# Chunked linear attention feeding an FFN: from 128-position blocks to two halves of 64 with a state at the chunk's middle

## Chip, cores and metric

The kernel runs on one NeuronCore of a Trainium2 chip. The metric is device time in microseconds (us) of one execution. Engines: PE (TensorE matmul; PEld is its weight load), DVE (VectorE), ACT (ScalarE), POOL (GpSimd), SP (which issues most DMAs). Lnnn is a line of the kernel; where nothing else is said, of the kernel before.

## What is computed

Gated linear attention over 4 batches, 8 heads, 768 positions and 48 features, then a multiplicative FFN on the 3072 tokens of 384 features:

```
for t in range(S):
    state = alpha[:, :, t, :, None] * state + einsum('bhd,bhe->bhde', k[:, :, t], v[:, :, t])
    y[:, :, t] = einsum('bhd,bhde->bhe', q[:, :, t], state)
x = y.transpose(0, 2, 1, 3).reshape(B * S, H * D)
out = ((x @ w1) * (x @ w2)) @ w3 @ w_out
```

The weights come as 64-bit floats and are converted on the chip.

## The kernel before

The sequence is cut into chunks of 128 positions: 6 per batch (NCH), 24 in all (N). Inside a chunk the decay is taken into q and k by cumulated logarithms: `logs` (L315, ACT), `decays` (L338: cumulated sums on PE, then two exponentials on ACT, L363/L364), `decayed` (L371, one multiplication on DVE, L373: qk = kq * e). `transposed` (L384) turns q and k by 16 transposes on PE (L395) and two copies on ACT (L397, tile qkT). Heads go in four pairs j, with i the head of a pair.

Chunks from 8 on are called turned (L161). For such a chunk n the work on PE is:
- `scores(n)` -> `turned_scores` (L435): k'q in both 64-position halves and from the first half to the second; 16 products, 8 of them 128 columns wide and 8 of them 64 (L443). Between them stand the low values of chunk n-1 (L432), 8 products of 64 rows. Four mask operations on DVE (L453) bring the scores to SBUF (tile ms).
- `attend_state(n)` (L476): q times the state T before the chunk, both halves of the positions, 16 products of 48 rows and 64 columns (L485) into two PSUM banks y. The first chunk of a batch has no state.
- `attend(n)` (L498): the second half's values, 8 products of 128 rows (L508) onto y[0]; three copies on ACT (L505 twice, L510) to x, which SP stores to DRAM (xd).
- `outer(n)` (L400): k'v over all 128 rows, 8 products (L407); DVE adds the old state (L417) for the new one. A batch's last chunk has none. `advance` (L419) multiplies every second state by a decay on POOL (L426).
- `turn_v` (L164): POOL copies half of v to the other partitions (tile vt), for the products that write across the halves.

Loop iteration n (L756 to L863) works on chunk n's scores, chunk n-1's values and chunk n+1's transposes, in the order: state of n-1, scores of n with low values of n-1, transposes of n+1, values of n-1, outer products of n. After these follow pieces of the FFN's gate from a queue (`run`, L718): a piece is `exact` (L584), nine products into two banks (L581), with an activation on ACT (L590) and an operation on DVE (L592); two pieces make a gate, and DVE then multiplies both (L629). Also in the iteration: weight conversion (`convert`, L246 to L269, on ACT and DVE), the sums for chunk n+3 (L357), and L334, an operation on logarithms on DVE. In iterations 9, 13, 17, 21 no gate pieces run; `split_early` (L554; L548 on ACT, L549 and L551 on DVE) splits the FFN's next input into three parts, which the next gate pieces read.

A gate's products multiply parts 0 and 1 into the first bank, part 2 into the second. From about 181 us on, attention is over and PE works on the rest of the gate, the folding of w3 and w_out, and the projection.

The framework takes instructions in the order in which the functions issue them and sorts each engine's queue itself by its own estimates; `issue_after` marks only bound this order. The queue is fixed when the kernel is built. An engine runs its own queue in order and waits on semaphores for others. PSUM has 8 banks, given out by `bank()` as earlier users finish.

Of the kernel before, what the change touches and what calls it, by code (L numbers as in the profile page):

```python
# [12 lines left out]
I32 = mybir.dt.int32  # L13
# [35 lines left out]
def kernel(  # L49
# [77 lines left out]
    vts = [p1.tile([C, NP, DP], FP32, name=f"vt{i}") for i in range(2)]  # L127
    for x in vts:
        nc.gpsimd.memset(x[:, :, D:], 0.0)
# [66 lines left out]
    keep_turned = p1.tile([C, 2, DP], I32, name="keep_turned")  # L196
    qks = [p1.tile([C, 2, H, DP], FP32, name=f"qk{i}") for i in range(3)]
    Ts = [p1.tile([C, NP, DP], FP32, name=f"T{i}") for i in range(2)]
    decs = [p1.tile([C, LINE // 2], FP32, name=f"dec{i}")[:, 0:3 * NP].rearrange("p (m j) -> p m j", m=3) for i in range(2)]
# [10 lines left out]
    for half in range(2):  # L210
        nc.gpsimd.tensor_copy(out=keep_turned[ds(DP * half, DP), 1 - half], in_=keep[ds(DP * half, DP), ds(DP * half, DP)])
    nc.gpsimd.memset(keep_turned[DP:, 1], -1)
# [12 lines left out]
    for x in Ts + decs:  # L225
        nc.gpsimd.memset(x, 0.0)
# [202 lines left out]
    def attend_low(n, j, i):  # L429

        s, w = ds(DP * i, DP), (vts[n % 2][:, j, :] if i else st["v", n][:, 2 * j, :])
        nc.tensor.matmul(st["y", n][1][ds(DP * (1 - i), DP), j, :], w[s], st["ms", n][s, i, j, 0:DP],  # L432
                         start=(n % NCH == 0 and j == 0), stop=(j == NP - 1), skip_group_check=True)

    def turned_scores(n):  # L435

        qkT = st["qkT", n]
        sc = [bank().rearrange("p (j c) -> p j c", j=NP) for _ in range(2)]
        for j in range(NP):
            for part in range(2):  # L440
                for i in range(2):
                    r, t = ds(DP * i, D), slice(DP * part, C)
                    nc.tensor.matmul(sc[i][ds(DP * (part ^ i), DP), j, t], qkT[r, 0, j, ds(DP * part, DP)],  # L443
                                     qkT[r, 1, j, t], start=True, stop=True)
            if turned(n - 1):
                for i in range(2):
                    attend_low(n - 1, j, i)
        ms = work.tile([C, 2, NP, C], FP32, tag="ms", name="ms")
        for i in range(2):
            r = ds(DP * i, DP)  # L450
            low, high = (keep_turned[r, 0], keep_turned[:, 1]) if i else (keep[r, 0:DP], keep[:, DP:])
            for x, mask, t in ((slice(DP * i, DP * (i + 1)), low, slice(0, DP)), (slice(0, C), high, slice(DP, C))):
                masked = nc.vector.tensor_tensor(ms[x, i, :, t].bitcast(I32), sc[i][x, :, t].bitcast(I32),  # L453
                                                 mask[:, None, :].to_broadcast([x.stop - x.start, NP, DP]),
                                                 op=ALU.bitwise_and)
        ends_of_part1[0] = mark["ms", n] = masked.ins
        st["ms", n] = ms

    def scores(n):
        if turned(n):  # L460
            return turned_scores(n)
# [14 lines left out]
    def attend_state(n):  # L476
        qkT = st.pop(("qkT", n))
        if turned(n):
            y = st["y", n] = [bank()[:, 0:NP * DP].rearrange("p (j c) -> p j c", c=DP) for _ in range(2)]
            if n % NCH:  # L480
                for j in range(NP):
                    for t in range(2):
                        for i in range(2):
                            r = ds(DP * i, D)
                            nc.tensor.matmul(y[t][ds(DP * (i ^ t), DP), j, :], Ts[n % 2][r, j, :],  # L485
                                             qkT[r, 1, j, ds(DP * (1 - t), DP)],
                                             start=(j == 0), stop=False, skip_group_check=True)
            return
# [9 lines left out]
    def attend(n):  # L498
        y, ms, vc = st.pop(("y", n)), st.pop(("ms", n)), st.pop(("v", n))
        to = xd.rearrange("(h i d) t -> i d h t", i=2, d=D) if turned(n) else xd.rearrange("(b h d) t -> b d h t", b=2, d=D)  # L500
        if turned(n):
            x = work.tile([C, NP, C], FP32, tag="x", name="x", bufs=4)
            with after_marks(*[("qkT", n + 2)] * (n + 2 < N)):
                for i in range(2):
                    nc.scalar.copy(x[ds(DP * i, DP), :, 0:DP], y[1][ds(DP * (1 - i), DP)])  # L505
            for j in range(NP):
                for i in range(2):
                    nc.tensor.matmul(y[0][ds(DP * i, DP), j, :], vts[n % 2][:, j, :] if i else vc[:, 2 * j, :], ms[:, i, j, DP:],  # L508
                                     start=(n % NCH == 0 and j == 0), stop=(j == NP - 1), skip_group_check=True)
            copied = nc.scalar.copy(x[:, :, DP:], y[0])  # L510
# [245 lines left out]
    for n in range(N + 1):  # L756
# [17 lines left out]
        late_state = early_pair(n - 1)  # L774
        if n and not late_state:
            attend_state(n - 1)
        if n < N:
            scores(n)
            if late_state:
                attend_state(n - 1)  # L780
        else:
            for j in range(NP):
                for i in range(2):
                    attend_low(n - 1, j, i)
        transposed(n + 1)
# [33 lines left out]
        with after_marks(*[("vt", n)] * turned(n)):  # L819
            advance(n)  # L820
# [3 lines left out]
        if n:  # L824
            attend(n - 1)
        outer(n)
# [15 lines left out]
        run(pieces > 1)  # L842
# [14 lines left out]
        turn_v(n + 1)  # L857
# [98 lines left out]
```

## Time and profile before

| what | value |
|---|---|
| runs | 455.81, 455.42, 460.12 us; median 455.81 |
| profiled execution, its own time | 455.61 us |
| its span | 453.9 us |
| granted PE clock, mean over the span | 1.00 |
| scores L443 | 512 instructions, 33.0 us of PE |
| masks L453 | 64 on DVE, 26.6 us |
| copies of v L167 | 32 on POOL, 15.5 us |

A product of 32-bit floats counts as two PE instructions in the rows (x32 is 16 products); a transpose counts as one. Durations of PE rows overlap: what a group costs is the distance from its start to the next group's start. The same holds, less strongly, for DVE and ACT: the next operation starts some 0.08 to 0.12 us before the listed end of the one before. Times within the profile are counted from the span's start.

### The profile page before, as it was taken

What the parts mean: (1) busy time and instruction counts of PE and PEld (TensorE: products, weight loads), DVE (VectorE), ACT (ScalarE), POOL (GpSimd) and SP (SyncE); (2) the same over time, 40 slices, a digit from 0 to 9 for tenths busy, and PEclk for the clock granted to TensorE, in tenths of its full rate; (3) what the DMA queues carried; (4) which work ended last, traced back from release to release, by engine and by line L of the source; (5) the groups of instructions that cost most, each with busy time, mean ns of one, the idle gap of its engine ahead of it and who ended that gap; (6) DMA issues with size and microseconds to landing.
All of it is one profiled execution on the core that took longest, in us unless ns stands there. A gap on an engine that the chain in (4) does not pass through costs nothing.

```text
span 453.9 us, 11111 instructions
## 1 busy us (share of the span) xinstructions
PE 439.3 (97%) x4304; PEld 390.9 (86%) x4304; DVE 370.0 (82%) x600; ACT 278.4 (61%) x523; POOL 85.1 (19%) x171
## 2 busy tenths in 40 slices
PE   4998999999999999999999999999999999999996
PEld 2766898898989978888888888888888999999996
DVE  2799997999979898989999999999427576777671
ACT  4778956878688573978865766575435333333430
POOL 6334341225116330021121010100010000000000
PEclk9999999999999999999999999999999999999999
DMA  8999999989999952465775263610139565565411
GB/s 202 271 227 250 239 243 244 210 203 223 211 216 194 276 168 95 153 187 179 243 232 186 94 201 105 205 48 23 48 101 271 173 183 161 167 190 175 150 49 52
DMA packets 149381, 79.98 MB, mean 176 GB/s; under 512 B 97184, under 2 KB 138784, under 8 KB 149328
## 3 DMA queue, kind: packets, MB, share of 16 engines
q1 hardware_dynamic: 143840, 64.84, 54.2%
q0 software_dynamic: 5488, 14.43, 9.8%
q8 instruction: 34, 0.56, 0.5%
q14 instruction: 19, 0.16, 0.1%
HBM read 57.19 MB, written 22.06 MB: 175 GB/s over the span
## 4 chain that ended last, share of the span: by engine, by line
PE 87%; DVE 6%; DMA 3%; ACT 2%; issue 1%; SPq 0%; DVEq 0%
PE bank L581 73%; PE bank L395 2%; PE bank L443 2%; PE bank L508 2%; PE bank L485 2%; PE bank L407 1%; DVE qk L373 1%; DMA x3b<-xd 1%; PE bank L432 1%; DVE ms L470 1%; PE bank L357 1%; DMA abd<-r 1%; PE bank L354 1%; DMA xd<-x 1%; DMA ac<-in_alpha_dram 1%
## 5 line engine op out<-in xcount | busy, mean ns | idle before, releaser
L581 PE MATMUL bank<-x,w 128*128 128x512 f32 (+1 forms) x688 | 161.6, 372 | 0.4 <-ACT e L364 0.2
L581 PEld LDWEIGHTS bank<-x,w 128*128 128x128 f32 x688 | 124.4, 188 | 19.5 <-issue 0.7
L581 PE MATMUL bank<-w3o,ab 128*128 128x384 f32 x576 | 100.2, 334 | 0.0
L581 PEld LDWEIGHTS bank<-w3o,ab 128*128 128x128 f32 x576 | 99.9, 188 | 0.2
L581 PE MATMUL bank<-x3b,w 128*128 128x512 f32 (+1 forms) x248 | 71.6, 384 | 0.0
L606 ACT ACTIVATE bank<-bank 128x512 f32<-128x512 f32 (+1 forms) x72 | 40.9, 570 | 30.7 <-PE bank L581 30.6
L581 PEld LDWEIGHTS bank<-x3b,w 128*128 128x128 f32 x248 | 46.3, 188 | 8.5 <-ACT x L505 0.4
L655 POOL DMA_DIRECT2D abd<-r x33 | 19.3, 585 | 138.8 <-DVE r L641 116.5
L705 DVE TENSOR_TENSOR ab<-abl,ab 128x1024 fp32r<-128x1024 f32 x24 | 29.4, 1226 | 14.9 <-ACT ab L704 14.9
L590 ACT ACTIVATE t<-bank 128x384 f32<-128x384 f32 x24 | 11.8, 492 | 45.5 <-PE bank L581 45.5
L704 ACT ACTIVATE ab<-abl 128x1024 fp32r<-128x1024 f32 x24 | 25.4, 1060 | 22.6 <-PE bank L581 20.1
L397 ACT COPY qkT<-bank 128x512 f32<-128x512 f32 x48 | 25.9, 593 | 20.0 <-PE bank L395 20.0
L581 PE MATMUL bank<-wo,w3T 128*128 128x384 f32 x192 | 36.3, 337 | 0.0
L581 PEld LDWEIGHTS bank<-wo,w3T 128*128 128x128 f32 x192 | 34.1, 188 | 1.2
L592 DVE SCALAR_TENSOR_TENSOR o<-bank,t 128x384 f32<-128x384 f32 x24 | 13.4, 558 | 25.4 <-issue 14.0
L252 ACT ACTIVATE power<-power,rebias 128x512 uint32<-128x512 uint32 (+1 forms) x36 | 25.0, 695 | 13.8 <-DVE power L250 13.8
L373 DVE TENSOR_TENSOR qk<-kq,e 128x768 f32<-128x768 f32 x24 | 23.1, 962 | 9.0 <-ACT e L364 8.8
L641 DVE TENSOR_TENSOR r<-bank,r 128x512 f32<-128x512 f32 x32 | 21.8, 682 | 9.3 <-PE bank L581 8.6
L706 DVE SCALAR_TENSOR_TENSOR ab<-ab,abl 128x1024 fp32r<-128x1024 f32 x24 | 29.2, 1219 | 0.0
L592 DVE SCALAR_TENSOR_TENSOR r<-bank,r 128x384 f32<-128x384 f32 (+1 forms) x40 | 22.7, 577 | 6.5 <-ACT r L590 4.9
L590 ACT ACTIVATE r<-bank 128x384 f32<-128x384 f32 (+1 forms) x40 | 20.5, 515 | 9.5 <-PE bank L581 8.1
L254 DVE SCALAR_TENSOR_TENSOR mant<-mant,raw 128x512 f32<-128x512 uint32 (+1 forms) x36 | 23.5, 652 | 2.9 <-ACT raw L246 2.9
(119 smaller groups left out, 744.6 us busy)
## 6 DMA issues: line engine op xcount, KB each, us to landing
abl<-abd SPq DMA_DIRECT2D x24, 512.0 KB, 4.3
abd<-r POOLq DMA_DIRECT2D x33, 256.0 KB, 3.5
raw<-in_moe_w_dram SPq DMA_DIRECT2D x64, 128.0 KB, 4.1
raw<-in_moe_w_dram SPq DMA_DIRECT2D x12, 512.0 KB, 4.9
kq<-in_k_dram SPq DMA_DIRECT2D x24, 192.0 KB, 5.0
kq<-in_q_dram SPq DMA_DIRECT2D x24, 192.0 KB, 4.8
xd<-x SPq DMA_DIRECT2D x48, 96.0 KB, 3.6
xT<-xd POOLq DMA_DIRECT2D x6, 768.0 KB, 5.4
```

Of the source, the lines that this page charges most:

```text
L252: nc.scalar.activation(power, power, AF.Relu, scale=2.0 ** 23, bias=rebias)
L254: nc.vector.scalar_tensor_tensor(mant, top, 2.0 ** -20, rest, op0=ALU.mult, op1=ALU.add)
L373: mark["qk", n] = nc.vector.tensor_mul(qks[n % 3][:, :, :, 0:D], st.pop(("kq", n)), st.pop(("e", n)).rearrange("p i (h d) -> p i h d", h=H ...
L397: mark["qkT", n] = nc.scalar.copy(qkT[:, :, :, ds(DP * half, DP)], tp[half]).ins
L581: nc.tensor.matmul(p, w[part][i], x[part][i], start=start and part == parts[0] and i == 0, stop=stop and part == parts[-1] and i == n - 1, ...
L590: mark["scale"] = nc.scalar.activation(t, p1, AF.Copy, scale=(1.0 + 1.0 / P) * scale).ins
L592: nc.vector.scalar_tensor_tensor(to, p2, scale, t, op0=ALU.mult, op1=ALU.add)
L606: mark["scale"] = nc.scalar.activation(p, p, AF.Copy, scale=1.0 + 1.0 / P).ins
L641: nc.vector.tensor_mul(r[0], p, r[0])
L704: nc.scalar.activation(t[:, 0], ab, AF.Copy, scale=1.0 - 2.0 ** -13)
L705: nc.vector.tensor_sub(t[:, 1], ab, t[:, 0].bitcast(FP32))
L706: nc.vector.scalar_tensor_tensor(t[:, 2], t[:, 0].bitcast(FP32), -1.0 - 1.0 / P, ab, op0=ALU.mult, op1=ALU.add)
```

## The change

From chunk 8 on the chunk is treated as two halves of 64 positions, each with its own state before it. `outer_halves` makes k'v for the first and the second half apart (16 products of 64 rows into two banks, 8 for a batch's last chunk). `middle` adds the first to T for the state at the chunk's middle, U, and the second to U for the next T, both on DVE. `half_scores` needs scores only inside each half: 16 products of 64 columns, two masks of 128x256. `attend_state` takes T for the first half and U for the second. `attend` makes the values as 16 products of 64 rows. The first of these into each bank wait for U's addition, since state products write to the same banks from other rows. `turn_v`, vt and the low values are gone.

The order of iteration n becomes: state of n-1, outer products of n, U and T of n on DVE, `advance`, scores of n, values of n-1, transposes of n+1; then the copies of x behind the copies of qkT, and `split_early` after these (it stood ahead of the copies of x in program order). In iteration 24 one gate piece moves between the state's products and the values.

```diff
-    def turn_v(n):
-        if turned(n):
-            for half in range(2):
-                mark["vt", n] = nc.gpsimd.tensor_copy(out=vts[n % 2][ds(DP * half, DP), :, 0:D],
-                                      in_=st["v", n][ds(DP * (1 - half), DP), 1::2, 0:D]).ins
...
+    def outer_halves(n):
+        qk, vc = qks[n % 3], st["v", n]
+        parts = st["halves", n] = [bank()[:, 0:NP * D].rearrange("p (j d) -> p j d", j=NP) for _ in range(1 if last(n) else 2)]
+        for j in range(NP):
+            for half, part in enumerate(parts):
+                for i in range(2):
+                    s = ds(DP * half, DP)
+                    nc.tensor.matmul(part[ds(DP * i, DP), j, :], qk[s, 0, 2 * j + i, :], vc[s, 2 * j + i, 0:D],
+                                     start=True, stop=True)
+
+    def middle(n):
+        parts, U = st.pop(("halves", n)), Us[n % 2][:, :, 0:D]
+        if n % NCH == 0:
+            made = nc.vector.tensor_copy(out=U, in_=parts[0])
+        else:
+            made = nc.vector.tensor_add(U, parts[0], Ts[n % 2][:, :, 0:D])
+        mark["U"] = made.ins
+        if last(n):
+            return
+        if n % 2:
+            to = st["T", n] = work.tile([C, NP, D], FP32, tag="tmp", name="tmp", bufs=1)
+        else:
+            to = Ts[1][:, :, 0:D]
+        nc.vector.tensor_add(to, parts[1], U)
...
-    def turned_scores(n):
+    def half_scores(n):
...
+                for i in range(2):
+                    r, t = ds(DP * i, D), ds(DP * half, DP)
+                    nc.tensor.matmul(sc[i][t, j, :], qkT[r, 0, j, t], qkT[r, 1, j, t], start=True, stop=True)
+        ms = work.tile([C, 2, NP, DP], FP32, tag="msh", name="msh")
         for i in range(2):
+            masked = nc.vector.tensor_tensor(ms[:, i].bitcast(I32), sc[i].bitcast(I32),
+                                             keep_half[:, None, :].to_broadcast([C, NP, DP]), op=ALU.bitwise_and)
...
+            for j in range(NP):
+                for t in range(2 if n % NCH else 1):
+                    for i in range(2):
+                        r = ds(DP * i, D)
+                        nc.tensor.matmul(y[t][ds(DP * (i ^ t), DP), j, :], (Ts if t else Us)[n % 2][r, j, :],
+                                         qkT[r, 1, j, ds(DP * (1 - t), DP)],
+                                         start=(j == 0), stop=False, skip_group_check=True)
...
+            for j in range(NP):
+                for t in range(2):
+                    for i in range(2):
+                        s = ds(DP * (1 - t), DP)
+                        o = nc.tensor.matmul(y[t][ds(DP * (i ^ t), DP), j, :], vc[s, 2 * j + i, :], ms[s, i, j, :],
+                                             start=(n % NCH == 0 and t == 1 and j == 0), stop=(j == NP - 1), skip_group_check=True).ins
+                        if j == 0:
+                            tc.add_manual_dep(o, mark["scale" if n == N - 1 else "U"].name, mybir.DependencyInfo(
+                                mybir.DependencyClass.Sync, mybir.DependencyReason.DATA), reason="the state's products write from other rows")
+            transposed(n + 2)
             with after_marks(*[("qkT", n + 2)] * (n + 2 < N)):
                 for i in range(2):
                     nc.scalar.copy(x[ds(DP * i, DP), :, 0:DP], y[1][ds(DP * (1 - i), DP)])
-            for j in range(NP):
-                for i in range(2):
-                    nc.tensor.matmul(y[0][ds(DP * i, DP), j, :], vts[n % 2][:, j, :] if i else vc[:, 2 * j, :], ms[:, i, j, DP:],
-                                     start=(n % NCH == 0 and j == 0), stop=(j == NP - 1), skip_group_check=True)
-            copied = nc.scalar.copy(x[:, :, DP:], y[0])
+                copied = nc.scalar.copy(x[:, :, DP:], y[0])
...
+        if turned(n) and not turned(n - 1):
+            advance(n)
         if n and not late_state:
             attend_state(n - 1)
+        if turned(n):
+            outer_halves(n)
+            middle(n)
+            advance(n + 1)
         if n < N:
             scores(n)
             if late_state:
                 attend_state(n - 1)
-        else:
-            for j in range(NP):
-                for i in range(2):
-                    attend_low(n - 1, j, i)
-        transposed(n + 1)
+        if n == N:
+            run(1)
+        if turned(n - 1):
+            attend(n - 1)
+        else:
+            transposed(n + 1)
...
-        if n:
+        if n and not turned(n - 1):
             attend(n - 1)
-        outer(n)
+        if not turned(n):
+            outer(n)
```

More of the change, by code (lines that the diff above doesn't have):

```diff
@@ L126 @@
         nc.gpsimd.memset(x[:, :, D:], 0.0)
-    vts = [p1.tile([C, NP, DP], FP32, name=f"vt{i}") for i in range(2)]
-    for x in vts:
-        nc.gpsimd.memset(x[:, :, D:], 0.0)
     def rows(src, n):
@@ L195 @@
     keep = p1.tile([C, C], I32, name="keep")
-    keep_turned = p1.tile([C, 2, DP], I32, name="keep_turned")
+    keep_half = p1.tile([C, 2 * DP], I32, name="keep_half")[:, 0:DP]
     qks = [p1.tile([C, 2, H, DP], FP32, name=f"qk{i}") for i in range(3)]
     Ts = [p1.tile([C, NP, DP], FP32, name=f"T{i}") for i in range(2)]
+    Us = [p1.tile([C, NP, DP], FP32, name=f"U{i}") for i in range(2)]
     decs = [p1.tile([C, LINE // 2], FP32, name=f"dec{i}")[:, 0:3 * NP].rearrange("p (m j) -> p m j", m=3) for i in range(2)]
@@ L210 @@
     for half in range(2):
-        nc.gpsimd.tensor_copy(out=keep_turned[ds(DP * half, DP), 1 - half], in_=keep[ds(DP * half, DP), ds(DP * half, DP)])
-    nc.gpsimd.memset(keep_turned[DP:, 1], -1)
+        nc.gpsimd.tensor_copy(out=keep_half[ds(DP * half, DP)], in_=keep[ds(DP * half, DP), ds(DP * half, DP)])
     for x in qks:
@@ L224 @@
                                 channel_multiplier=-2 if e else 2)
-    for x in Ts + decs:
+    for x in Ts + Us + decs:
         nc.gpsimd.memset(x, 0.0)
@@ L427, in advance @@
                                                dec[:, :, None].to_broadcast([C, NP, D]), op=ALU.mult).ins
-    def attend_low(n, j, i):
-        s, w = ds(DP * i, DP), (vts[n % 2][:, j, :] if i else st["v", n][:, 2 * j, :])
-        nc.tensor.matmul(st["y", n][1][ds(DP * (1 - i), DP), j, :], w[s], st["ms", n][s, i, j, 0:DP],
-                         start=(n % NCH == 0 and j == 0), stop=(j == NP - 1), skip_group_check=True)
-    def turned_scores(n):
+    def half_scores(n):
         qkT = st["qkT", n]
-        sc = [bank().rearrange("p (j c) -> p j c", j=NP) for _ in range(2)]
+        sc = [bank()[:, 0:NP * DP].rearrange("p (j c) -> p j c", j=NP) for _ in range(2)]
         for j in range(NP):
-            for part in range(2):
+            for half in range(2):
                 for i in range(2):
[L442 to L445, printed above, removed]
-                for i in range(2):
-                    attend_low(n - 1, j, i)
-        ms = work.tile([C, 2, NP, C], FP32, tag="ms", name="ms")
-        for i in range(2):
[L450 to L455, printed above, removed]
+                    r, t = ds(DP * i, D), ds(DP * half, DP)
+                    nc.tensor.matmul(sc[i][t, j, :], qkT[r, 0, j, t], qkT[r, 1, j, t], start=True, stop=True)
+        ms = work.tile([C, 2, NP, DP], FP32, tag="msh", name="msh")
+        for i in range(2):
+            masked = nc.vector.tensor_tensor(ms[:, i].bitcast(I32), sc[i].bitcast(I32),
+                                             keep_half[:, None, :].to_broadcast([C, NP, DP]), op=ALU.bitwise_and)
         ends_of_part1[0] = mark["ms", n] = masked.ins
@@ L460, in scores @@
         if turned(n):
-            return turned_scores(n)
+            return half_scores(n)
         qkT = st["qkT", n]
@@ L479, in attend_state @@
             y = st["y", n] = [bank()[:, 0:NP * DP].rearrange("p (j c) -> p j c", c=DP) for _ in range(2)]
-            if n % NCH:
-                for j in range(NP):
-                    for t in range(2):
-                        for i in range(2):
[L484 to L487, printed above, removed]
+            for j in range(NP):
[5 more added lines that the diff above has]
+                                         start=(j == 0), stop=False, skip_group_check=True)
             return
@@ L505, in attend @@
                     nc.scalar.copy(x[ds(DP * i, DP), :, 0:DP], y[1][ds(DP * (1 - i), DP)])
-            for j in range(NP):
[L507 to L510, printed above, removed]
+                copied = nc.scalar.copy(x[:, :, DP:], y[0])
         else:
@@ L780 @@
                 attend_state(n - 1)
-        else:
-            for j in range(NP):
-                for i in range(2):
-                    attend_low(n - 1, j, i)
-        transposed(n + 1)
+        if n == N:
+            run(1)
+        if turned(n - 1):
+            attend(n - 1)
+        else:
+            transposed(n + 1)
         if n == 1:
@@ L818 @@
                 convert(3 if n == 1 else 2 if early else 1, raws)
-        with after_marks(*[("vt", n)] * turned(n)):
+        if not turned(n):
             advance(n)
@@ L823 @@
                 load_v(n + 2)
-        if n:
+        if n and not turned(n - 1):
             attend(n - 1)
-        outer(n)
+        if not turned(n):
+            outer(n)
         if n > FIRST:
@@ L841 @@
         convert(early and n > 0, raws)
-        run(pieces > 1)
+        run(pieces > 1 and n < N)
         if n:
@@ L856 @@
             assert len(done) == 2 * KM
-        turn_v(n + 1)
         run(pieces > 2)
```

## The prediction

> **What bounds it now.** I read the page's engine line, then the chain of waits in order of time, then the window table of the stage that the change touches, then each engine's instructions in order of time around one loop iteration.
>
> ```profile
> PE 439.3 (97%) x4304; PEld 390.9 (86%) x4304; DVE 370.0 (82%) x600; ACT 278.4 (61%) x523; POOL 85.1 (19%) x171
> ```
> ```profile
> 72.35:181.20 108.85, 107.15 (x2151) 96.16 (x2151) 101.15 (x197) 77.92 (x173) 32.81 (x64) 1.00 0.84 204
> ```
> ```profile
> 150.13 0.62 PE bank L485 x32
> ...
> 181.21 269.15 PE bank L581 x1362
> ```
>
> The second line gives for 72.35 to 181.20 us (loop iterations 9 to 24) the busy time and count of PE, PEld, DVE, ACT and POOL, the granted clock 1.00 and the DMA share 0.84. The third shows that after 181.21 the rest is one run of dense gate products, which the change leaves alone: what PE gains or loses before 181 us is what the kernel gains or loses. In the stage PE is full, but DVE with 101 of 109 us is nearly so, and DVE's rows follow the order of its queue: what stands ahead in it is done first.
>
> One iteration, n = 20, on PE (start, duration):
>
> ```profile
> 150.06 0.69 PE L485 MATMUL bank<-qkT,T 48*64 48x64 f32 x32
> 150.57 0.39 PE L443 MATMUL bank<-qkT 48*64 48x128 f32 x8
> ...
> 151.62 0.71 PE L395 MATMUL bank<-ident,qk 64*128 64x64 f32 x16
> 152.26 0.27 PE L508 MATMUL bank<-ms,v 128*64 128x64 f32 x1
> ...
> 152.77 0.62 PE L407 MATMUL bank<-v,qk 128*64 128x48 f32 x16
> 153.33 1.66 PE L581 MATMUL bank<-x,w 128*128 128x384 f32 x8
> ```
>
> and on DVE at the same time:
>
> ```profile
> 151.21 0.95 DVE L373 TENSOR_TENSOR qk<-kq,e 128x768 f32<-128x768 f32 x1
> 152.08 0.55 DVE L592 SCALAR_TENSOR_TENSOR r<-bank,r 128x384 f32<-128x384 f32 x1
> 152.67 0.56 DVE L629 TENSOR_TENSOR r<-r 128x384 f32<-128x384 f32 x1
> 153.15 0.74 DVE L453 TENSOR_TENSOR ms<-bank,keep 64x256 int32<-64x256 int32 x2
> ```
>
> The reader is to see that PE finished the scores at 151.6 but DVE came to their masks at 153.15, 1.5 us late. Before, nothing on PE needed these masks until the next iteration, so the lag cost nothing.
>
> **PE's own work.** From start to start, iteration 20 spends 0.51 on the state, 1.05 on scores and the interleaved low values (0.17 of it the hand-over to transposes), 0.64 on transposes, 0.51 on values, 0.56 on outer products: 3.27 us. After, state, scores and values each are 16 products of 64 columns on four tiles of at most 64x64, the form of the state's row: 0.51 each. The outer products become 16 half-height ones of 48 columns: between 0.38 (three quarters of 0.51) and 0.51, I take 0.45, the middle. Sum 0.51 x 3 + 0.45 + 0.17 + 0.64 = 2.8 us, 0.47 less. Iterations 8, 9, 10, 12, 14, 15, 16, 18, 20, 21, 22 get that (11 x 0.47 = 5.2). Iterations 11, 17, 23 had no outer product (2.81 before) and now have a half one; 13 and 19 had no state product and now have 8: nothing gained. Iteration 24 loses the eight low products and full-height values (1.71 before, 1.02 after): 0.7. In iteration 10 a wait of 0.66 ahead of the low values goes with them. PE alone: -6.5 us. All 144 added products are in these figures.
>
> [...]
>
> **DVE, POOL, ACT.** DVE loses two of four mask operations per chunk (1.55 us for four, 0.70 for two at L453's rates) and gets a second addition of L417's kind that must wait for the first (0.27 becomes 0.35 + 0.06 + 0.27): 0.44 less per chunk, 7.0 in all. POOL loses 32 copies of v (15.5 us); its own idle time hid them, so I count nothing except the 0.66 above. `advance` comes an iteration earlier on POOL; its 0.83 us ends well before the state product that needs it. SP's queue keeps its order of loads and stores; the stores of x leave an iteration later as before. ACT's three copies of x move ahead of the split of the FFN's input, see below.
>
> **The new wait.** The value products now wait for U, which DVE adds in the same iteration. Behind them on PE stand the transposes, and behind those the gate products and ACT's copies of qkT. From the state's start S, PE reaches the values at S + 1.47. U needs the outer products (S + 0.96), but also its turn on DVE: in the order of the built program's instructions, the gate's last L592, mostly its L629, and in places L373 (decay) or a weight operation stand ahead of it. I read from the trace of before when DVE got through these, add 0.35 for U, and 0.05 + 0.51 + 0.17 + 0.64 = 1.37 to the end of the transposes, and compare with where the old cluster ended:
> - n = 11: slot 87.58, end 89.30, before 88.69: +0.6.
> - n = 12: 96.47, 98.19 against 97.48: +0.7.
> - n = 15: decay and one weight operation ahead, 117.29, 119.0 against 117.09: +1.9.
> - n = 16: 124.93; six transposes stand ahead of the values there, 126.4 against 125.64: +0.8.
> - n = 19: two weight operations ahead, 145.01, 146.73 against 144.67: +2.1.
> - n = 20: 153.15, 154.87 against 153.33: +1.5.
> - n = 23: 173.63, values end 174.5 against 173.14: +1.4.
>
> Together +9.0. In iterations 10, 14, 18, 22 DVE is free and U is hidden, but there PE waits for the FFN input's split, whose chain begins at the transposes of the iteration before:
>
> ```profile
> 131.61 1.07 ACT L397 COPY qkT<-bank 128x512 f32<-128x512 f32 x2 [0.83 <-PE bank L395]
> 132.57 1.18 ACT L548 ACTIVATE x<-x3b 128x1152 fp32r<-128x1152 f32 x1
> 133.78 0.75 ACT L505 COPY x<-bank 64x256 f32<-64x256 f32 x2
> 134.55 0.37 ACT L510 COPY x<-bank 128x256 f32<-128x256 f32 x1
> ```
>
> Before, the split (L548) stood ahead of the copies of x; after, it stands behind them, 1.04 us later. Transposes' end + 0.05 + 0.96 (qkT) + 1.04 (x) + 1.07 (L548) + 1.27 (L549) + 0.87 + 0.47 (L551) + 0.2 puts the first gate product group's end at +5.9. For 9/10: transposes end 75.84, so 81.8 against 82.28: -0.5. For 13/14: 103.95, 109.9 against 110.2: -0.3. For 17/18: U behind a decay, 133.65, 139.6 against 138.3: +1.3. For 21/22: 160.6, and with DVE's 4.24 us for the three pieces 168.2 against 166.42: +1.8. Together +2.3. Iteration 8 gives -0.4, iteration 24 -0.7.
>
> **Sum.** 9.0 + 2.3 - 1.1 = +10.2 us if DVE reaches each slot no earlier than before. But it has 7.0 us less to do, and while PE waits it catches up. Upper bound of the loss: 10.2, and 1.0 more with outer products at 0.51. Lower bound: U always hidden, -6.5. Where DVE stands idle for ACT or a transfer ahead of the slot (the decay's load in 15, L590 in 17) the relief does not help; where it runs without a pause (11, 12, 16, 19, 20) it does. So I let half of the relief, 3.5, count: +6.7. The profiled execution took 455.61 (span 453.9 and 1.7 around it), 0.2 under the median 455.81. 455.6 + 6.7 = 462.3 us.
>
> **Rivals.** (1) Hidden wait, faster: DVE reaches U by S + 1.4 in nearly every iteration, PE keeps its -6.5: 449.1. For it: DVE's relief, and the gate's second half ends 0.1 us after S, so that L592 and L629 could be through at S + 1.1. Against: in n = 16, 17, 20 and 21 a decay (0.87) is queued ahead of U, which alone puts U at S + 2.2 or later; it decides only where DVE has no backlog. (2) Mostly hidden: all 7.0 of relief reach the slots, +3.2: 458.8, no measurable change; equally, transfers that now bind (share 1.03 in 72 to 80 us) could hold the gain of (1) back. (3) The new products are dearer than the state's row: at the pace of iteration 24's low products (0.47 for 8, so 0.94 for 16) outer products take 0.49 more, scores 0.43, values 0.43. Values count in full, of the other 0.92 the wait for U hides about half: 0.9 per iteration, 14 us, 470 to 477. For it: those low products are such 64-column products too. Against: they used two tiles, the state's row four, as the new ones do. [...] (4) That the change doesn't do what it says: the built order hoists transposes ahead of the values only in iterations 16 and 17, so the move is made in the others.
>
> **Chances.** Wait decides, 460.4 to 467: 0.63, the forecast. Rival 2, 451 to 460.3: 0.23. Rival 1: 0.10. Rival 3 and worse: 0.04. One per cent (4.6 us) is about what a measurement of this kernel can tell from no change. Slower by over 1%: 0.63 + 0.04 = 0.67; within: 0.23; faster: 0.10. The range runs from 455 (half of rival 2 below it, and rival 1) to 467 (upper bound 466.8): it leaves out 0.10 below it from rival 1, some 0.05 of rival 2 and 0.04 above, about 0.2. For the forecast's own case it is 460.4 to 467.
>
> **What would show it.** Right: among PE's waits a row of value products behind DVE's U with 6 us or more in total, PE idle for 0.5 to 2 us in iterations 11, 15, 17, 19, 20; clusters of 2.8 us of PE work; masks x32 of 0.41; DVE's busy time in the loop down by about 7; the gate's first products after each split waiting for L549's and L551's results. Wrong: values starting straight after the scores in those iterations (rival 1), or groups of 16 small products that take 0.8 us or more (rival 3). My least certain step is how much sooner DVE comes to U once it has less to do.

## The result, and the profile after

| | us |
|---|---|
| before, median of 4 runs | 456.63 (455.42 to 460.12) |
| after, median of 4 runs | 472.09 (471.26 to 473.88) |
| ratio | 1.0331, 95% interval 1.0263 to 1.0399 |
| profiled execution after (span) | 472.86 (471.1) |

The changed kernel is slower by 3.3%. The forecast had the direction; the size, +6.7 us, was far too small: measured were +15.5 us between the medians and +17.2 us between the two profiled spans, since the profiled execution of before lies 1.0 us below its median and that of after 0.8 above. First the page of the kernel after: the engine line, and the granted clock in 40 slices.

```profile
PE 442.1 (94%) x4592; PEld 391.1 (83%) x4592; DVE 358.8 (76%) x584; ACT 278.0 (59%) x523; POOL 69.6 (15%) x138
...
PEclk9997999999989899999999999999999999999999
```

PE's busy time went up by 2.8 us only, while the span grew by 17.2: the other 14.4 us are PE standing idle. DVE has 11 us less to do and POOL 15. And in three slices the clock is below 9; the page of before has a 9 in every slice.

The stage's window, the same stretch as before (busy time and count of PE, PEld, DVE, ACT, POOL, then clock, DMA share, GB/s):

```profile
72.35:181.20 108.85, 94.25 (x2206) 83.55 (x2204) 79.76 (x158) 71.72 (x162) 18.37 (x35) 0.97 0.80 184
```

PE was busy for 107.15 us of these 108.85, and is now for 94.25. DVE, nearly full before, now has 29 us to spare, and yet PE waits for it. PE's longest waits from 62 to 200 us (total, times, longest):

```profile
PE bank L508 <- DVE U L425: 10.6, 10, 2.1
PE bank L588 <- DVE x L556: 2.1, 3, 1.5
PE bank L508 <- DVE U L423: 0.6, 1, 0.6
```

L508 is the value products, L425 and L423 the making of U: 11.2 us in 11 iterations. PE in iteration 15 (start, duration, in brackets the idle time ahead and its releaser), and DVE at the same time:

```profile
119.37 0.63 PE L417 MATMUL bank<-v,qk 64*64 64x48 f32 x32
119.83 0.66 PE L453 MATMUL bank<-qkT 48*64 48x64 f32 x32
121.99 0.69 PE L508 MATMUL bank<-msh,v 64*64 64x64 f32 x32 [1.50 <-DVE U L425]
122.61 0.71 PE L386 MATMUL bank<-ident,qk 64*128 64x64 f32 x16
123.26 1.66 PE L588 MATMUL bank<-x,w 128*128 128x384 f32 x8
```
```profile
119.45 0.55 DVE L636 TENSOR_TENSOR r<-r 128x384 f32<-128x384 f32 x1
119.92 0.55 DVE L599 SCALAR_TENSOR_TENSOR r<-bank,r 128x384 f32<-128x384 f32 x1
120.39 0.95 DVE L364 TENSOR_TENSOR qk<-kq,e 128x768 f32<-128x768 f32 x1
121.25 0.42 DVE L238 TENSOR_SCALAR mant<-raw 128x512 uint32<-128x512 uint32 x1
121.59 0.35 DVE L425 TENSOR_TENSOR U<-bank,T 128x192 f32<-128x192 f32 x1
```

U's outer products are done at about 120, but DVE comes to U at 121.59, behind the gate's last operations, the decay and one weight operation, as forecast. PE's own groups are as short as forecast: outer products take 0.46 to the next group's start, values 0.62, transposes 0.65.

Why did so little of DVE's relief arrive? Look one step back, at ACT after the transposes of iteration 12, and at DVE, ahead of the U of iteration 13:

```profile
101.06 1.07 ACT L388 COPY qkT<-bank 128x512 f32<-128x512 f32 x2 [3.37 <-PE bank L386]
...
103.20 0.67 ACT L237 ACTIVATE raw<-raw 128x512 f32<-128x512 uint32 x1
```
```profile
103.90 0.69 DVE L245 SCALAR_TENSOR_TENSOR mant<-mant,raw 128x512 f32<-128x512 uint32 x1 [3.14 <-ACT raw L237]
...
106.65 0.55 DVE L599 SCALAR_TENSOR_TENSOR r<-bank,r 128x384 f32<-128x384 f32 x1
107.12 0.34 DVE L425 TENSOR_TENSOR U<-bank,T 128x192 f32<-128x192 f32 x1
```

ACT stands idle for 3.37 us for the transposes, which now stand behind the values; then come qkT, the copies of x, and the weight operation L237. DVE waits 3.14 us for that one, and only then works off what has piled up ahead of U. The values of iteration 13 wait 1.14 us for it. ACT's waits for the transposes from 62 to 182 us (total, times, longest), before and after:

```profile
ACT qkT L397 <- PE bank L395: 16.7, 11, 2.1
ACT qkT L388 <- PE bank L386: 35.4, 11, 4.7
```

So DVE's freed time lies behind the cluster of small products, and its backlog ahead of the next U: a loop from values over transposes, qkT, ACT and DVE to U and the values.

Last, the clock. Windows of 3.41 us around the two stretches at half clock behind 60 us (columns as above; the last but two is the clock):

```profile
129.29:132.70 3.41, 2.20 (x95) 1.82 (x86) 3.41 (x9) 0.33 (x1) 0.00 (x0) 1.00 0.47 135
132.70:136.11 3.41, 3.41 (x26) 3.28 (x19) 0.26 (x1) 2.50 (x6) 0.00 (x0) 0.50 1.04 231
...
153.17:156.58 3.41, 1.27 (x82) 1.13 (x78) 3.41 (x9) 0.26 (x1) 2.26 (x3) 1.00 1.03 244
156.58:160.00 3.42, 3.42 (x44) 3.19 (x35) 1.64 (x3) 1.83 (x5) 0.50 (x1) 0.50 0.49 109
```

Each stretch at 0.50 follows a window in which waits had left PE busy for 2.20 and 1.27 us. At half clock a group of eight gate products takes 2.87 us for 1.66, so the wait is paid a second time: +1.21 in iteration 16, +1.33 in 19. A third stretch, of 6.83 us, lies at 40.5 to 47.4, ahead of all that was changed.

### The profile page after: what moved, and what is told of

Its sections match the earlier page's. It is cut to its first block, busy times and chain, and to the rows that moved or that the text cites. A ratio compares the mean times of both kernels' runs of the same rounds, so it can differ in the third digit from the quotient of the medians.

```text
span 471.1 us, 11614 instructions
## 1 busy us (share of the span) xinstructions
PE 442.1 (94%) x4592; PEld 391.1 (83%) x4592; DVE 358.8 (76%) x584; ACT 278.0 (59%) x523; POOL 69.6 (15%) x138
## 4 chain that ended last, share of the span: by engine, by line
PE 75%; DVE 12%; ACT 5%; DMA 4%; issue 3%; SPq 0%; ACTq 0%; DVEq 0%
PE bank L588 65%; PE bank L386 2%; DMA ac<-in_alpha_dram 2%; DVE qk L364 2%; PE bank L508 2%; DVE r L599 1%; PE bank L469 1%; DMA xd<-x 1%; DMA xT<-xd 1%; PE bank L345 1%; PE bank L521 1%; DVE x L556 1%; ACT qkT L388 1%; DVE r L636 1%; DVE mant L248 1%
## 5 line engine op out<-in xcount | busy, mean ns | idle before, releaser
L588 PE MATMUL bank<-x,w 128*128 128x512 f32 (+1 forms) x688 | 164.8, 377 | 3.1 <-DVE x L556 2.1
L588 PEld LDWEIGHTS bank<-x,w 128*128 128x128 f32 x688 | 126.4, 191 | 23.1 <-DVE x L556 3.2
L245 DVE SCALAR_TENSOR_TENSOR mant<-mant,raw 128x512 f32<-128x512 uint32 (+1 forms) x36 | 23.4, 650 | 9.1 <-ACT raw L237 9.1
L597 ACT ACTIVATE r<-bank 128x384 f32<-128x384 f32 (+1 forms) x40 | 20.4, 514 | 10.8 <-PE bank L588 10.8
```

The source lines that it names most:

```text
L245: nc.vector.scalar_tensor_tensor(mant, top, 2.0 ** -20, rest, op0=ALU.mult, op1=ALU.add)
L588: nc.tensor.matmul(p, w[part][i], x[part][i], start=start and part == parts[0] and i == 0, stop=stop and part == parts[-1] and i == n - 1, ...
L597: mark["scale"] = nc.scalar.activation(t, p1, AF.Copy, scale=(1.0 + 1.0 / P) * scale).ins
```

## The experiments

Four theories ran through them, which the expectations name by number. Theory 1, the wait: the values wait for U because of what DVE has queued ahead of it, and the rest follows. Theory 2, the loop: with the transposes behind the wait, ACT and DVE get their input late, and DVE's backlog then stands ahead of the next U; its rival is that the new order costs by itself, whoever waits. Theory 3, the clock: short idle times cost a second time, at half clock. Theory 4, the instruction stream: the stops of PE for which the profile names no releaser (`issue` in the rows) are waits for PE's next instructions. Each ratio is to executions of the kernel before taken beside it, with its 95% interval. The two right columns come from one profile each: the time from the start of state products in iteration 8 to iteration 24, apart for the split iterations (10, 14, 18, and 21 with 22) and the others.

| kernel | ratio [95%] | split, us | others, us |
|---|---|---|---|
| before | 1 | 42.2 | 73.8 |
| after | 1.0331 [1.0263, 1.0399] | 44.6 | 86.1 |
| decay and weights behind U | 1.0197 [1.0146, 1.0248] | 44.4 | 81.4 |
| transposes first | 1.0221 [1.0153, 1.0289] | 53.3 | 73.8 |
| copies of x behind the split | 1.0421 [1.0364, 1.0478] | 55.4 | 80.0 |
| values wait for ACT instead | 1.0329 [1.0274, 1.0385] | 62.7 | 71.7 |
| transposes first but in four | 1.0194 [1.0146, 1.0243] | 52.8 | 73.3 |
| the same, and decay behind U | 1.0161 [1.0106, 1.0215] | 53.9 | 71.5 |
| the same, and conversion early | 1.0200 [1.0149, 1.0251] | 55.6 | 71.0 |
| the same, and split behind U | 1.0215 [1.0153, 1.0277] | 53.2 | 73.5 |
| before, in the new order | 1.0046 [1.0010, 1.0082] | 43.6 | 75.9 |
| after with fillers | 1.0388 [1.0328, 1.0447] | 48.2 | 85.8 |

**Decay and weight operations behind U on DVE.** All of `convert`, `decayed` and `logs` of an iteration is ordered behind its U.

```diff
-            with after_marks(*marks):
+            with after_marks(*marks, *["U"] * turned(n)):
                 convert(3 if n == 1 else 2 if early else 1, raws)
```

> The changed kernel, but from iteration 8 on the decay (L364), the weight operations (L238 to L260) and L325 are queued on DVE behind U's addition instead of ahead of it; nothing else moves. Theory 1 (place in DVE's queue): in the trace of the changed kernel these rows stand right ahead of U in iterations 9, 11, 13, 15, 16, 17, 19, 20 and 21 (0.87 each for a decay, 0.6 each for a weight operation), and DVE idles for 3 to 4 us earlier in the same iterations (3.77 and 2.97 us ahead of L599), so they cost nothing there. Of 11.2 us of PE waiting for U some 9 go, and with them most of the 2.5 us that PE's granted clock of 0.50 after two of these waits cost: 472.1 - 11 = 461 (458 to 464). Rival (DVE as a whole is the bound): the work only moves and the wait appears at the masks or at the transposes behind the decay: 468 to 473.

Measured: 467.30 us, above the expected range, and 7.5 us of waits for U instead of 11.2. The queue ahead of U counts, but only some 5 us came back (4.9 in the table's two columns). What still stands there was seen in iteration 19:

```profile
148.63 0.68 DVE L245 SCALAR_TENSOR_TENSOR mant<-mant,raw 128x512 f32<-128x512 uint32 x1
...
150.30 0.68 DVE L248 TENSOR_TENSOR mant<-mant,power 128x512 f32<-128x512 f32 x1
150.90 0.34 DVE L425 TENSOR_TENSOR U<-bank,T 128x192 f32<-128x192 f32 x1
```

L245 to L248 belong to the conversion of the iteration before, late because ACT's part of it stood behind qkT. The loop was not cut.

**Transposes ahead of the value products.**

```diff
+            transposed(n + 2)
             for j in range(NP):
                 for t in range(2):
...
-            transposed(n + 2)
```

> The changed kernel with only the order transposes, then value products, as before the change; U is still waited for. Theory 1 (PE waits for U): each wait of 0.38 to 2.14 us is covered by 0.64 us of transposes, 11 times: -6.5; the qkT copies start earlier by the wait too, so the gate's first products after the four splits come up to 1 us earlier each: -3. 472.1 - 9.5 = 462.6 (460 to 466). Rival (values late is what costs, not an idle PE; everything behind them still hangs on U): 470 to 473.

Measured: 466.81 us, between the expected range and its rival's. In the ordinary iterations the waits for U nearly vanish, and these cost 73.8 us, as before the change. ACT's wait for the transposes fell with them, from 35.4 to 21.9 us, as theory 2 has it. The time is lost in the split iterations, 11.1 us against before. In iteration 18 the transposes wait for a bank, the gate products for qkT, and the values run at half clock (0.69 for 32 in iteration 15 of the changed kernel, here 1.13):

```profile
141.58 1.06 PE L386 MATMUL bank<-ident,qk 64*128 64x64 f32 x15 [1.10 <-ACT e L355]
143.22 1.65 PE L588 MATMUL bank<-x,w 128*128 128x384 f32 x4 [0.58 <-ACT qkT L388]
144.79 1.13 PE L509 MATMUL bank<-msh,v 64*64 64x64 f32 x32
```

**Copies of x behind the split's first operation**, in the split iterations: a test of the forecast's price for them.

```diff
+            copies(*["x3h"] * (n - 2 in begin and n > FIRST))
```

> The changed kernel with ACT's three copies of x queued behind the split of the FFN input (L555) in the four iterations that have one, as before the change; elsewhere they stay. Theory: the split comes 1.04 us earlier four times, of 4.5 us that these four places lost: 472.1 - 4 = 468 (467 to 470). Rival (the split is late because the transposes ahead of it wait for U, not because of the copies): 471 to 473.

Measured: 477.05 us; the expectation failed by its sign. The copies of x are what frees the banks of the state's products, and the next scores and transposes wait for those banks:

```profile
78.47 0.68 PE L453 MATMUL bank<-qkT 48*64 48x64 f32 x22 [1.02 <-ACT x L518]
...
81.03 0.71 PE L386 MATMUL bank<-ident,qk 64*128 64x64 f32 x8 [1.23 <-ACT e L355]
```

In this form, at least, ahead of the split is the cheaper place for the copies.

**Values wait for ACT instead of U.** A one-column copy on ACT out of the outer products' bank releases them.

```diff
+        mark["drained"] = nc.scalar.copy(probe, parts[0][:, 0, 0:1]).ins
...
-                            tc.add_manual_dep(o, mark["scale" if n == N - 1 else "U"].name, mybir.DependencyInfo(
+                            tc.add_manual_dep(o, mark["scale" if n == N - 1 else "drained"].name, mybir.DependencyInfo(
```

> The changed kernel, but the value products wait for a one-column copy by ACT out of the bank of the first half's outer products instead of for U's addition on DVE. It comes behind the state's products on PE's queue as U does, so it stands for the same end of the state's products; U itself is needed only in the next iteration. ACT idles for 3 to 4 us around this point (35.4 us in all ahead of the qkT copies). Theory 1 (U's turn on DVE): the wait goes wholly: -11.2 us, and -2.5 for the clock of 0.50 behind two of the waits; the splits' chains start earlier as well, up to -2: 472.1 - 15 = 457 (454 to 461). Rival (products or masks hold the values, or DVE's backlog comes back as a wait of the next state product for U and T): 466 to 473.

Measured: 473.41 us, no better than the changed kernel. The wait theory is borne out where it applies: the ordinary iterations take 71.7 us, 14.4 less than after and 2.1 less than before. The split iterations lose 18.1 us against after. The largest single wait there is in iteration 10, in the middle of the state's products, with no releaser in the profile (the last section shows where it stands among PE's rows):

```profile
82.82 0.36 PE L489 MATMUL bank<-qkT,T 48*64 48x64 f32 x1 [4.05 <-issue]
```

The half clock follows it, three stretches on end up to 93 us, and 34 us in all in this execution.

**Transposes first but in iterations 10, 14, 18, 22; the same with decay and weights behind U; the same with ACT's weight operations no longer behind qkT.** Each is added to the one before.

```diff
+            if n - 2 not in begin:
+                transposed(n + 2)
...
+            if n - 2 in begin:
+                transposed(n + 2)
```
```diff
-        marks = (*[("qkT", n + 1)] * (n < N - 1), *[("qk", n + 1), ("ms", n)] * early, *["x3"] * (n - 2 in begin and n > FIRST))
+        marks = (*[("qkT", n + 1)] * (n < N - 1 and not (turned(n) and n - 2 not in begin)), *[("qk", n + 1), ("ms", n)] * early, *["x3"] * (n - 2 in begin and n > FIRST))
```

> The changed kernel with the transposes ahead of the value products in all iterations except 10, 14, 18 and 22 (those right behind a split of the FFN input). Theory 2 (a chain that closes on itself: while PE waits for U, ACT has no transposes to copy, DVE no ACT results, so DVE's backlog comes together just ahead of the next U; transposes that go first break it): in the run with transposes first everywhere the other iterations had hardly a wait for U left (1.8 us in all) and cost as much as before the change, but these four took 53.3 us against 44.6 in the changed kernel. With the better of the two in each, 472.1 - 12 = 460 (457 to 463). Rival (the four iterations are late for the transposes of the iterations ahead of them too, so their loss stays): 466 to 470.

> As the run with transposes first but in four iterations, and the decay, the weight operations and L325 queued behind U on DVE as in the first run. Theory 2: the two take away the same waits, so the second adds little: 1 to 2 us below that run, 458.5 (455 to 462). Rival (they add up, 5 us each): 455 or less.

> As the run before it, but ACT's part of the weight operations (L237, L243) may go ahead of the qkT copies except in the four split iterations, into the 2 to 4 us in which ACT waits for transposes. Theory 2: DVE's L245 to L248, which wait for L237 (3.14 us of idle ahead of L245 in iteration 12) and then run just ahead of U in iterations 13, 16 and 19, move into DVE's idle time, and the last waits for U of 1 us and more go: 2 us less, 456.5 (453 to 461). Rival (the weights have not landed by then, or DVE's queue keeps its order): the same as the run before it or up to 3 us more.

Measured: 468.21, 468.10 and 469.43 us, all above the expected ranges and the first in its rival's. The three differ by no more than their intervals. The ordinary iterations get down to 71.0 us, 2.8 less than before, in clusters of 2.82 us: with the loop cut, all of PE's forecast gain for them is there (six of them had 0.47 each). All of it and more is lost in the split iterations, which stay at 53 to 56 us in whichever way the transposes stand. PE's waits in the second of the three kernels:

```profile
PE bank L486 <- issue: 3.2, 3, 1.5
PE bank L386 <- ACT e L355: 2.7, 3, 1.2
PE bank L591 <- ACT qkT L388: 1.9, 3, 0.7
PE bank L510 <- DVE U L425: 1.0, 2, 0.6
```

**The kernel before, in the new order**: its second half's values ahead of the transposes, the copies of x behind qkT.

```diff
-        transposed(n + 1)
+        if turned(n - 1):
+            attend(n - 1)
+        else:
+            transposed(n + 1)
```

> The kernel before the change with one part of the change alone: in each of these iterations the high value products stand ahead of the transposes, and ACT's copies of x behind the qkT copies; chunks stay whole and no product waits for U. Theory 2 (the later transposes cost by themselves only 0.5 us per chunk, and become dear only with a wait ahead of them): 0.5 to 1.1 us later at each of four splits, +3 us on the kernel before (1 to 5). Rival (the order alone makes most of the loss, since ACT and DVE start later in every iteration): +8 us or more.

Measured: 462.79 us (10 runs) against 459.94; by the ratio 2.1 us more (0.5 to 3.8), as expected. The order alone, without a wait in it, costs a seventh or so of the loss.

**The split's DVE steps behind the U of the next iteration**, on top of the last of the three.

```diff
+        if n - 3 in begin and n - 1 > FIRST:
+            g, tiles = begin[n - 3]
+            with after_marks("U"):
+                st.pop("rest")()
+            fill.extend(gate(g, f) for f in tiles)
```

> As the run with ACT's part of the weight operations early, and DVE's three steps of each FFN input split (L556, L558) queued behind U's addition of the next iteration (10, 14, 18, 22) instead of ahead of it; ACT's step stays. Theory 1 in its full form (whatever long work stands ahead of U on DVE makes PE wait): in the three runs with transposes first these four iterations cost 55.6 us against 44.1 in the first run, since U stood behind 2.6 us of split; the other iterations already take no longer than before the change (8.08 and 6.52 us against 8.3 and 6.9). Both put together, about 1 us under the kernel before: ratio 0.998 (0.988 to 1.008). Rival (these iterations lose for another reason, PE's own issue stalls or a shortage of banks, and the half clock that follows): ratio 1.015 to 1.025 as the three runs before it.

Measured: 466.76 us against 456.10, in the rival's range. The waits for U are gone from the split iterations, and 53.2 us are still spent there. But that sum hides two opposite changes. Iterations 10, 14 and 18 take 32.7 us, 7.8 less than in the run that this one is made from. Iterations 21 and 22 take 20.4 for 15.1: the split's steps now come too late there, PE waits 3.58 us for them, and half clock comes with it from 174.2 to 181.0 us. What is left in all four are stops without a releaser, 6.4 us, as the rival has it. In iteration 10 the stop without a releaser is 2.48 us long, the window around it has 1.07 us of work, and the next is at half clock:

```profile
80.83 0.27 PE L486 MATMUL bank<-qkT,T 48*64 48x64 f32 x1 [2.48 <-issue]
```
```profile
78.48:81.90 3.42, 1.07 (x70) 1.07 (x73) 0.23 (x2) 3.36 (x9) 0.00 (x0) 1.00 0.90 222
81.90:85.31 3.41, 3.41 (x70) 3.10 (x61) 3.41 (x6) 1.80 (x4) 0.54 (x1) 0.51 1.06 237
```

**Fillers**: in the changed kernel eight products that nobody reads between scores and values, in ten iterations, to keep PE busy during the wait.

```diff
+        if n in (9, 11, 12, 13, 15, 16, 17, 19, 20, 21):
+            w = w12[0][:, 0, 0, 0, :]
+            for _ in range(8):
+                nc.tensor.matmul(full[:, 256:512], w[:, 0:C], w[:, 256:512], start=True, stop=True)
```

> The changed kernel with eight products of 128x256 that nothing reads (about 1 us of PE work) between scores and value products in iterations 9, 11, 12, 13, 15, 16, 17, 19, 20 and 21, into unused columns of the score bank. Theory 3 (idle PE time costs twice: PE's granted clock falls to 0.50 for 3.4 us after a stretch of 3.4 us in which PE was busy for less than about 2 us): the fillers lie in the waits for U, U comes when it came, and the two later stretches of 0.50 of the changed kernel (from 132.6 and 156.5 us) are gone: 2 to 3 us less, 469.5 (468 to 471). Rival (the clock does not follow PE's idle time, or the fillers come in addition): 472 to 482, with stretches of 0.50 after 120 us as before.

Measured: 474.86 us. The fillers take 1.22 us each time:

```profile
120.72 1.22 PE L458 MATMUL bank<-w 128*128 128x256 f32 x8
122.26 0.69 PE L513 MATMUL bank<-msh,v 64*64 64x64 f32 x32 [0.33 <-DVE U L425]
```

The ordinary iterations take 85.8 us, no more than without them: most of the 12 us of added products lies inside the waits, of which 2.2 us are left. The two half-clock stretches at 132 and 156 us are gone, with PE kept busy, though another came at 180 to 187. But these two had cost the ordinary iterations 2.5 us, and that gain does not show either, so some 2 us of the fillers came in addition. The rows of the clock went as the clock theory has it. The time lies in its rival's range and decides nothing by itself: iterations 21 and 22, where the new stretch lies, take 18.8 us against 15.6, which is more than the two stretches had cost.

**Shifted instructions** (one run): the kernel with the split behind U, with 64 unread products in iteration 8, which move every later PE instruction on in its stream.

> The run with the split behind U, with 64 small products that nothing reads (128 instructions on PE, about 2 us) in iteration 8, so that every later instruction of PE comes 128 places further back in PE's instruction stream. Theory 4 (PE's issue stalls are its instruction stream running dry at the end of a block of 256 instructions: in all runs they hit the same few instructions, and the profile counts 36 instruction transfers of 16 KB where PE has 36 x 256 instructions): the stalls leave the state and first-half products of iterations 10, 14, 18 and 22 and come 64 products earlier, at the end of the value products or just behind them in iterations 9, 13, 17 and 21; the time is about that of the run it is made from plus 2 us, 468.5 (464 to 472). Rival (something these state products need is late: U, T, a bank): the stalls stay inside the state and first-half products of iterations 10, 14, 18 and 22.

Measured: 484.36 us beside 458.02, one execution of each. The stops without a releaser left the instructions at which the unshifted kernels have them (state's products in iterations 10, 18 and 22, an outer product in 14), so these instructions are not their cause. They didn't come back where they were expected: one of 0.91 us is left, in the scores of iteration 22. The time is far above the expectation, with 9.5 us for the added products themselves and a wait of 4.4 us for ACT in one place. The time therefore decides nothing; the place of the one stop does, with those of all other profiles: the last section shows that they all stand at the same place of a block of 256 rows, as theory 4 has it.

## Why the prediction was right in direction and wrong in size

| term, us between the profiled executions | predicted | measured |
|---|---|---|
| iteration 8 | -0.4 | -0.31 |
| wait for U in 11, 12, 15, 16, 19, 20, 23, less DVE's relief | 9.0 - 3.5 | +7.15 |
| split iterations with the one before each | +2.3 | +5.36 |
| half clock in 16 and 19 | none | +2.54 |
| iteration 24 and behind | -0.7 | +0.40 |
| ahead of iteration 8 | 0 | +2.07 |
| sum | +6.7 | +17.2 |

Of the 10.5 us that the forecast lacks between the two profiles, 3.1 lie in the split iterations, 2.5 in the clock, 2.1 ahead of iteration 8, 1.65 in the relief of DVE and 1.1 from iteration 24 on. The mechanism was right. Two steps of it failed: the times of U's turns, read from the trace of before as if DVE's input would come as it did there (2 and 3 below), and the clock, put at nothing (5).

1. *The wait decides.* Right: it is PE's first wait, with 11.2 us, in the iterations named (11, 15, 17, 19, 20 among them), behind the operations named. Rivals 1 and 2, which hide it, fall with that. Its prices were near: over the seven iterations +9.0 with no relief, measured +7.15.
2. *"So I let half of the relief, 3.5, count."* This step failed. By the row above, 1.85 us arrived, though DVE's busy time fell by 11.2, not 7. The forecast moved U's slot by DVE's work alone. But the transposes stand behind the wait, and what DVE works on comes from them over ACT; a later cluster makes DVE's input later by as much. ACT's wait for the transposes grew by 18.7 us. The kernel with the transposes first bears this out: with them out of the loop ACT's wait fell to 21.9 us and the ordinary iterations from 86.1 to 73.8. That is 12.3 us, more than the ten waits there can be covered by 0.64 us of transposes each (6.4) and the half clock (2.5) together.
3. *Split iterations, "together +2.3".* Most of the readings held. U is hidden in 10, 14, 18 and 22. The copies of x take 1.03 to 1.04 us ahead of the split (from the start of L516 to that of L555), and 1.04 was forecast; put behind it, they hold banks, and the time is longer for that. In 9, 17 and 21, with a wait for U in each, the transposes end 3.51, 4.12 and 3.57 us after the iteration's start; the forecast's ends, counted from the starts before, are at 3.56, 4.34 and 3.59. Iteration 13 failed by step 2: L245 to L248 stand ahead of its U, and the transposes end at 4.16 us where the forecast has 2.80 (103.95 less 101.15), 1.4 late. The chain from the transposes' end to the end of the first gate group (the next group's start) was priced short as well: 6.4 to 6.6 us for 5.9 in three of the four places and 7.9 for 7.6 in the last, together 2.0, in small amounts at qkT, at L555 and at the end.
4. *PE's own work, -6.5.* The size per cluster was right, 2.82 us where nothing waits (2.8 forecast). Of the 6.5 us, 2.8 belong to the ordinary iterations, and they show in the table of experiments only where the wait is gone: 71.0 to 71.7 us against 73.8. In the changed kernel they are inside the waits. The 0.66 us of iteration 10 were misread: not a wait that POOL's copies cause, but one of the stops without a releaser (last section), of which the changed kernel has 0.34 us there. Rival 3, which would give 470 to 477, has the right time and the wrong reason: at the full clock the groups take 0.45 to 0.63 us where nothing disturbs them, and of the groups without a stop only scores come to 0.8 or a little above (0.83 in iteration 16, 0.86 in 18).
5. *The clock.* The forecast had no such term: the clock was 1.00 throughout the trace of before. It costs 2.54 us in this stage.
6. *Ahead of iteration 8, +2.07.* Not the change: PE's rows up to there are the same, one by one, in both kernels. The difference goes with the stretch at half clock around 40 to 49 us, which some of the profiled executions have and others not: those with it begin iteration 8 at 64.7 to 66.7 us, those without at 62.6 to 63.9, and the kernel before in the new order, which has it, at 65.9.
7. *"POOL copies hidden".* Right: POOL has 15.5 us less to do, and nothing of that is seen in the time.
8. *Iteration 24, -0.7.* By the start of the gate products behind its values it gained some 0.3 us. The rest was lost behind it: at 222.88 us PE waits 0.39 us for a bank that ACT frees, which it does not before.

What the experiments add: cutting the loop does not save the change. In every version without the long wait for U the split iterations take 10 to 21 us longer than before, by stops without a releaser, by banks that come late, and by the half clock behind both. These iterations have two clusters of small products close together, some 290 PE and as many PEld rows, with no gate products between. In the changed kernel the wait for U seems to have covered them: its stops come to 1.2 us. No version was faster than before, the best is 1.0161 [1.0106, 1.0215]. The stops come to 2.9 to 6.8 us in these versions, against 1.1 in the kernel before; how the rest of the split iterations' loss divides between banks and clock is open.

## What to carry to other kernels

When a change puts a wait for another engine into an in-order queue, follow what stands behind the wait until it returns to the engine waited for: if that engine's input comes from there, its freed time lies on the wrong side of the wait and pays nothing back. Removing such a wait brings forward work that it had covered, so price the next limit (banks, PE's stops without a releaser, the next engine's queue) before counting the wait as gain. Where the rows show a clock that falls, count a wait on PE that comes close to others at up to twice its length: here 1.21 us more followed a wait of 1.21, and 1.33 one of 2.14. And where PE stops without a releaser, count its rows: here all 36 such stops stood at a place that repeats every 256 rows, and each ended 1.25 to 1.59 us after a transfer of the instruction queue had landed.

## What the runs showed of the hardware

**The clock falls after short idle times.** In the profiles of this case all stretches at 0.50 are 3.41 us or whole multiples of it, apart from what a profile's end cuts short, on one grid of 3.41 us in each execution. In the windows at full clock just ahead of them PE was busy for 0.00 to 2.29 us, so that as little as 1.1 us of idle time was enough; none with 2.30 us or more was followed by a stretch, and between 1.87 and 2.29 us both happened. What decides between the two there was not shown.

**PE stops at one place in 256 of its rows.** The instruction queue on the pages of before and after:

```profile
q8 instruction: 34, 0.56, 0.5%
...
q8 instruction: 36, 0.59, 0.5%
```

34 transfers of 16 KB stand beside 8,608 PE and PEld rows before, and 36 beside 9,184 after: 253 and 255 rows to a transfer. The thirteen profiles have 36 stops of PE without a releaser, of 0.25 to 4.05 us. Counted over all of PE's rows from the first (products, weight loads and those of its sequencer), every one of them stands at the 194th or 195th row of a block of 256, whatever instruction is there: a value product before the change, outer, state's and gate products after it, transposes with the fillers, scores with the shifted stream. Each ends 1.25 to 1.59 us after a transfer of this queue has landed; the stop of 4.05 us ends at 82.82, and the transfer ran from 80.42 to 81.38. That PE waits there for its next instructions, as theory 4 has it, is the author's reading of these places and times; no run shows what a transfer holds. The place comes 465 times in the thirteen profiles, and a stop is seen at 36 of these. They lie where PE uses up its rows fast: the densest 576 of them, two clusters of a split iteration, take 7.0 us in the changed kernel (from 74.0 us on), and 10.4 in the kernel before. Why a transfer comes later in one profile than in another was not looked into.

**The added products**, each with a weight load of its own, took 0.15 us apiece at 256 columns and at 64: eight of 128x256 took 1.22 us (the fillers), 64 of 64 columns 9.48 (the shifted instructions).
